# TensorE's row flags as one word of eight bits, made beside the last routing and loaded ahead of expert 0's last rows

## The chip, the cores and the metric

One core of a Trainium2 chip runs the whole program once. The metric is device time in microseconds (us). The engines are TensorE (PE in the profile, with its weight loads as PEld), VectorE (DVE), ScalarE (ACT), GpSimd (POOL) and SyncE (SP). Each runs its own list of instructions in order, and a sequencer in front of each engine reads that list: it resolves branches, loads and computes registers, and waits for semaphores.

## The reference, cut to what matters

Three steps follow each other: a gated linear attention, a dense layer, and a layer of eight experts, in which each of 3072 tokens goes to the one expert with the largest logit.

```
x = attention(q, k, v, alpha)                       # 3072 x 384
h = x @ w_in;  x = (h * cos(h)) @ w_out             # d_ff 2048
logits = x @ w_gate;  e_idx = argmax(logits, axis=1)
for e in range(8):
    mask = e_idx == e
    h  = max(x[mask] @ w1[e], 0)                    # 384 -> 1024
    ye = h @ w2[e]                                  # 1024 -> 384
    out[mask] = gate_w[mask] * eom[mask, e] * ye
```

How many tokens an expert gets is known only while the program runs.

## The kernel before

The dense layer works on groups of 512 tokens; the last one is group 5. After a group's second matmul stage the tokens are routed: `route_logits`, `route_rank` and `route_rows` (lines 488 to 541) compute for each token its row in the DRAM buffer `xs`, which has a region of rows for each expert, and keep in `base` the next free row of every expert. `route_send` scatters the rows with GpSimd's indirect DMA. After the last `route_rows`, `base - ebase` is the number of rows of each expert.

Then the experts run one after the other on up to 448 rows each (`CAP`). Expert 0 is split: its first 256 rows (`early`, written down as filled before the last group is routed) are worked on between the last routing's steps (`first(j)`, `second(j)`, lines 937 to 1003), and its last 192 rows (`r = begin(0)`) come after that: SP loads them (`load_rows`), PE transposes them (`rows_trans`, line 642), ACT and DVE split them into halves `exh` and `exl`, and the loop of line 1039 runs them as its first expert, with `e_stage1` for eight blocks `j` of nine matmuls each (line 671) and then `e_part2` for the row tiles.

An expert with at most 384 rows (`LOW`) needs less work. Whether it has that few is decided on the chip: `by_rows` (line 648) puts a branch on PE's sequencer ahead of each of the eight blocks of `e_stage1` and ahead of the 64-row tile of part two, nine branches an expert, 72 in all. The flag is in a register of PE. All eight registers are filled at line 1031: DVE computes `few` and `fewi` (lines 1023, 1026, 1030) after expert 0's last rows have been transposed, and PE loads the eight words with one load and then, for every word, two more sequencer instructions that check its bounds. The blocks of `e_stage1` write two PSUM banks in turn (`hp`), and DVE clears those two and a third one (`op`) at line 1037, just before the loop, after `fewi`.

The order is written by hand: `tc.manual_schedule` (line 937) keeps PE, ACT, DVE and SP in the order of the code, and each waits by semaphores for what it needs.

```
few_r = nc.values_load_multi_w_load_instructions(fewi[0:1, 0:E], engines=[ENG.PE], min_val=0, max_val=1)[1]
```

Of the kernel before, what the change touches and what calls it, by code (L numbers as in the profile page):

```python
# [8 lines left out]
F32 = mybir.dt.float32  # L9
F32R = mybir.dt.float32r  # L10
BF16 = mybir.dt.bfloat16
U32 = mybir.dt.uint32
# [38 lines left out]
CEB = CW8 + GU * E  # L51
CTOK = CEB + E
CROW = CTOK + NU
CCOL = CROW + 1


@with_exitstack
def kernel(
# [466 lines left out]
    def route_rows(g):  # L525
        oh, rp = rk.pop(g)
        t = s_p.tile([128, GU, E], F32, tag="rk", name="rk")
        nc.vector.tensor_tensor(
            out=t, in0=rp[:, 0], in1=base.rearrange("p (o e) -> p o e", o=1).to_broadcast([128, GU, E]), op=ALU.add
        )  # L530
        nc.vector.tensor_tensor(out=t, in0=t, in1=oh, op=ALU.mult)
        pf = s_p.tile([128, GU, 1], F32, tag="pf", name="pf")
        nc.vector.tensor_reduce(out=pf, in_=t, axis=AX.X, op=ALU.add)
        pu = s_p.tile([128, GU, 1], U32, tag="pu", name="pu")
        nc.vector.tensor_copy(pu, pf)
        nc.vector.tensor_tensor(out=base, in0=base, in1=rp[:, 1, 0], op=ALU.add)
        if g == NG - 2:

            nc.vector.tensor_scalar_max(base[:, 0:1], base[:, 0:1], float(EARLY))
        rk[g] = pu  # L540
# [404 lines left out]
    with tc.manual_schedule(engines={ENG.PE, ENG.Activation, ENG.DVE, ENG.SP}):  # L945
# [7 lines left out]
        def second(j):  # L953
            for t in range(n_t):
                e_part2(early, t, accs[t], j)
# [22 lines left out]
            x1_rows(g, s)  # L978
        route_rank(g)
        route_rows(g)  # L980
        for s in range(GU):
            route_send(g, s)
        second(1)
# [7 lines left out]
        second(5)  # L991
        first(7)
        second(6)
        m1.close()

        m2 = ExitStack()
# [12 lines left out]
        for t in range(n_t):  # L1009
# [2 lines left out]


        nt = o_p.tile([128, E + 1], F32, name="nt")
        few = o_p.tile([128, E], F32, name="few", bufs=1)
        fewi = o_p.tile([128, E], U32, name="fewi", bufs=1)
        nc.vector.tensor_tensor(out=nt[:, 0:E], in0=base, in1=ebase, op=ALU.subtract)
        nc.vector.tensor_scalar(
            out=nt[:, 0:E], in0=nt[:, 0:E], scalar1=float(127 - CAP), scalar2=127.0, op0=ALU.add, op1=ALU.max
        )  # L1020
        nc.vector.tensor_reduce(out=nt[:, E:E + 1], in_=nt[:, 0:E], axis=AX.X, op=ALU.max)

        nc.vector.tensor_scalar(
            out=few, in0=base, scalar1=float(LOW), scalar2=None, op0=ALU.subtract
        )
        nc.vector.tensor_tensor(out=few, in0=few, in1=ebase, op=ALU.is_le)
        nc.vector.tensor_copy(ntl, nt)
        nc.vector.tensor_scalar(out=ntl, in0=ntl, scalar1=7, scalar2=None, op0=ALU.logical_shift_right)

        nc.vector.tensor_copy(fewi, few)  # L1030
        few_r = nc.values_load_multi_w_load_instructions(fewi[0:1, 0:E], engines=[ENG.PE], min_val=0, max_val=1)[1]


        banks = [ps_h.tile([128, 512], F32, tag="h", name="hp") for _ in range(2)]
# [2 lines left out]
            nc.vector.memset(b, 0.0)  # L1037

        for e in range(E):
            r["few"], r["banks"] = few_r[e], banks  # L1040
            steps = load_expert(e + 1, vr_p if e % 2 else vl_p) if nxt else []

            def step():
                if steps:
                    for f in steps.pop(0):
                        f()

            hbs = []
            for j in range(NEF):

                n = r["n"]
                hb = h_p.tile([128, 2 * n], F32R, tag="hb", name="hb")
                e_stage1(r, j, hb[:, 0:n], [(slice(0, n - 64), hb[:, n + 64:]), (slice(n - 64, n), hb[:, n:n + 64])])
                hbs.append(hb)
                if j % 2:
                    step()
            r["gates"] = gates(z_p, r["xe"][:, :, DM:], len(r["tiles"]))
            n_t = len(r["tiles"])
            for i, t in enumerate((n_t - 1, *range(n_t - 1))):
                if i == n_t // 2 and nxt:  # L1060
                    rows_trans(nxt, z_p, "exh", "exl")
                step()
                if i == n_t - 1:
                    while steps:
                        step()
                ot = o_p.tile([128, DM], F32, tag="ot", name="ot")
                if r["tiles"][t] == 64:
                    op = e_acc(r, t, i, 128)
                    for m in by_rows(r.get("few"), (1, 0)):
                        if m:  # L1070
                            for j in range(NEF):
                                e_part2_both(r, t, op, j, hbs[j])
                    low = o_p.tile([64, DM], F32, tag="low", name="low", bufs=1)
                    nc.scalar.copy(low, op[64:128])
                    nc.vector.tensor_tensor(out=low, in0=op[0:64], in1=low, op=ALU.add)
                    op = low
                else:
                    op = e_acc(r, t, i)
                    for j in range(NEF):
                        e_part2(r, t, op, j)  # L1080
                e_out(r, t, op, ot)
            r = nxt
            nxt = begin(e + 2) if e + 2 < E else None
# [71 lines left out]
def _layout(inputs):  # L1155
# [32 lines left out]
    for n in range(NU):  # L1188
        c[:, CTOK + n] = (n % B) * S + (n // B) * C + perm
    c[:, CROW] = np.arange(128)  # L1190
    return {
        "units": u.reshape(NU, 128, UCOL),
        "cst": c,
# [26 lines left out]
```

## Time and profile before

| what | value |
|---|---|
| median of 3 runs | 814.5 us (813.9 to 815.12) |
| profiled execution, its own time | 812.32 us |
| its span, first to last instruction | 810.5 us |
| PE busy | 769.4 us (95%) |
| DVE, ACT, POOL busy | 501.9, 425.3, 316.6 us (62, 52, 39%) |
| mean granted TensorE clock | 0.981 of full speed |
| chain that ended last | PE 52%, issue 27%, DVE 11% |

Times are from the span's start. The last routing lies at 555 to 558 us, expert 0's last rows at 568 to 596 us, experts 1 to 7 behind them, and the end at 810.5 us. A granted clock of 1.00 is TensorE's 2.4 GHz, 0.50 its 1.2 GHz. An engine name with a q (PEldq, PEq, SPq) is the sequencer or queue in front of that engine.

### The profile page before, as it was taken

How to read it: one execution, taken by the hardware profiler on the slowest of the kernel's cores; microseconds unless marked ns; L12 is line 12 of the kernel's file. 1: busy time of each engine (PE TensorE's matmuls, PEld its weight loads, DVE VectorE, ACT ScalarE, POOL GpSimd, SP SyncE). 2: the span in 40 equal slices, each digit the busy share in tenths (PEclk: the TensorE clock that was granted, in tenths of full speed). 3: DMA queues.
4: the chain of work that ended last, by engine and by line, in shares of the span. 5: the costliest groups of instructions: out<-in, count | busy, mean ns of one | idle time of the engine just before them, and what ended most of it. 6: DMA issues, size and time to landing. Idle time of an engine off the chain costs nothing.

```text
span 810.5 us, 13963 instructions
## 1 busy us (share of the span) xinstructions
PE 769.4 (95%) x5346; PEld 655.7 (81%) x5346; DVE 501.9 (62%) x955; ACT 425.3 (52%) x782; POOL 316.6 (39%) x304
## 2 busy tenths in 40 slices
PE   8679899999999999999999999999699999999994
PEld 5557777888888888888888888889699999999994
DVE  8999998675467537663676334744565655655530
ACT  2454565754575457644665467555354545554420
POOL 3566756544355335543464424662011101101101
PEclk9998999999999999999999999999899999999998
DMA  9524452713201230113010101211565445645201
GB/s 326 205 94 159 170 199 100 243 60 112 80 1 54 73 125 1 54 59 109 31 55 20 41 0 59 89 50 44 182 192 181 135 142 176 191 123 159 67 13 34
DMA packets 46881, 85.31 MB, mean 105 GB/s; under 512 B 4152, under 2 KB 38488, under 8 KB 44240
## 3 DMA queue, kind: packets, MB, share of 16 engines
q1 hardware_dynamic: 43344, 74.67, 28.1%
q0 software_dynamic: 3456, 9.57, 3.2%
q8 instruction: 50, 0.82, 0.4%
q14 instruction: 31, 0.25, 0.1%
HBM read 69.01 MB, written 15.99 MB: 105 GB/s over the span
## 4 chain that ended last, share of the span: by engine, by line
PE 52%; issue 27%; DVE 11%; POOL 4%; DMA 2%; ACT 1%; POOLq 0%; SPq 0%; ACTq 0%; DVEq 0%
PE acc L418 22%; PE hp L379 21%; POOL out_dram L711 4%; DVE cv L347 3%; PE sc L211 2%; DMA un<-in_units_dram 2%; DVE cv L352 2%; PE yp L269 2%; PE yp L261 2%; DVE cv L356 2%; PE pp L285 1%; PE tp L442 1%; DVE t L397 1%; DVE t L392 1%; DVE w L151 1%
## 5 line engine op out<-in xcount | busy, mean ns | idle before, releaser
L405 POOL TENSOR_TENSOR gl<-t,gh 128x512 fp32r<-128x512 f32 x95 | 127.8, 1345 | 182.2 <-ACT gh L404 152.5
L386 ACT ACTIVATE t<-hp 128x512 f32<-128x512 f32 x96 | 57.3, 596 | 140.1 <-PE hp L379 130.4
L397 DVE TENSOR_TENSOR t<-hp,t 128x512 f32<-128x512 f32 x96 | 65.7, 684 | 89.3 <-ACT t L394 89.3
L392 DVE SCALAR_TENSOR_TENSOR t<-t,hp 128x512 f32<-128x512 f32 x96 | 65.7, 684 | 79.7 <-ACT t L386 79.6
L711 POOL DMA_INDIRECT out_dram<-ot,tk x32 | 31.3, 979 | 205.9 <-ACT ot L710 205.6
L687 PE MATMUL op<-h,hb 128*128 128x384 f32 x384 | 102.4, 338 | 1.7 <-PEq L654 1.7
L418 PE MATMUL acc<-gh,woh 128*128 128x512 f32 x288 | 90.3, 421 | 0.0
L677 DVE SCALAR_TENSOR_TENSOR hb<-hp,hb 128x64 fp32r<-128x64 f32 (+3 forms) x136 | 45.3, 372 | 70.1 <-ACT hb L675 70.0
L379 PE MATMUL hp<-xh,wih 128*128 128x512 f32 x288 | 83.6, 398 | 3.7 <-DVE t L397 3.1
L418 PE MATMUL acc<-gl,woh 128*128 128x512 f32 x288 | 84.2, 399 | 0.0
L418 PE MATMUL acc<-gh,wol 128*128 128x512 f32 x288 | 83.9, 399 | 0.0
L379 PE MATMUL hp<-xh,wil 128*128 128x512 f32 x288 | 82.6, 395 | 0.0
L379 PE MATMUL hp<-xl,wih 128*128 128x512 f32 x288 | 82.5, 395 | 0.0
L393 ACT ACTIVATE t<-t 128x512 f32<-128x512 f32 x96 | 60.7, 632 | 38.3 <-DVE t L392 38.3
L675 ACT ACTIVATE hb<-hp 128x448 fp32r<-128x448 f32 (+2 forms) x72 | 36.3, 504 | 72.3 <-PE hp L671 70.3
L599 DVE TENSOR_TENSOR l<-raw,h 128x768 fp32r<-128x768 f32 x60 | 57.3, 957 | 25.8 <-ACT h L595 25.0
L687 PEld LDWEIGHTS op<-h,hb 128*128 128x128 f32 x384 | 69.7, 188 | 3.0 <-issue 3.0
L394 ACT ACTIVATE t<-t,halfpi 128x512 f32<-128x512 f32 x96 | 69.6, 725 | 3.1
L379 PEld LDWEIGHTS hp<-xh,wih 128*128 128x128 f32 x288 | 54.4, 191 | 18.0 <-DVE t L397 2.2
L418 PEld LDWEIGHTS acc<-gh,wol 128*128 128x128 f32 x288 | 55.1, 191 | 13.4
L418 PEld LDWEIGHTS acc<-gl,woh 128*128 128x128 f32 x288 | 54.9, 191 | 12.8
L379 PEld LDWEIGHTS hp<-xl,wih 128*128 128x128 f32 x288 | 54.5, 189 | 12.9
(144 smaller groups left out, 1454.4 us busy)
## 6 DMA issues: line engine op xcount, KB each, us to landing
raw<-in_w_dram SPq DMA_DIRECT2D x64, 384.0 KB, 3.4
un<-in_units_dram SPq DMA_DIRECT2D x20, 1032.0 KB, 4.9
raw<-in_w_in_dram SPq DMA_DIRECT2D x16, 384.0 KB, 3.7
raw<-in_w_out_dram SPq DMA_DIRECT2D x16, 384.0 KB, 4.1
xs<-zrow SPq DMA_DIRECT2D x8, 591.0 KB, 5.8
xe<-xs SPq DMA_DIRECT2D x7, 591.0 KB, 5.1
un<-in_units_dram SPq DMA_DIRECT2D x4, 512.0 KB, 6.2
un<-in_units_dram SPq DMA_DIRECT2D x4, 256.0 KB, 6.8
```

The costliest lines, as they stand in the source:

```text
L379: nc.tensor.matmul(out=hp, lhsT=w[:, k, fs], rhs=x[:, k, :], start=(n == 0), stop=(n == 3 * KD - 1))
L386: nc.scalar.activation(out=t, in_=hps[g, j], func=ACTF.Copy, bias=MAGIC)
L392: nc.vector.scalar_tensor_tensor(out=t, in0=t, scalar=MAGIC, in1=hp, op0=ALU.subtract, op1=ALU.subtract)
L393: nc.scalar.activation(out=t, in_=t, func=ACTF.Abs)
L394: nc.scalar.activation(out=t, in_=t, func=ACTF.Sin, scale=-TWO_PI, bias=halfpi)
L397: nc.vector.tensor_tensor(out=t, in0=hps.pop((g, j)), in1=t, op=ALU.mult)
L405: eng.tensor_tensor(out=gl, in0=gf, in1=gh.bitcast(F32), op=ALU.subtract)
L418: nc.tensor.matmul(out=acc[g][k], lhsT=w[:, j, ks], rhs=a, start=(j == 0 and n == 0), stop=(j == NF - 1 and n == 2),)
L599: (nc.vector.tensor_tensor if i < 4 else sub)(out=lo, in0=raws[i], in1=h.bitcast(F32), op=ALU.subtract)
L677: nc.vector.scalar_tensor_tensor(out=out_, in0=hp[:, c], scalar=0.0, in1=hh[:, c].bitcast(F32), op0=ALU.max, op1=ALU.subtract)
L687: nc.tensor.matmul(out=op, lhsT=a[:, sl], rhs=w[:, j, :], start=(j == 0 and i == 0), stop=(j == NEF - 1 and i == 2))
L711: sent = nc.gpsimd.indirect_dma_start(out=out, out_offset=bass.IndirectOffsetOnAxis(ap=tk[0:n, t, :], axis=0), in_=ot[0:n], in_offset=None ...
```

## The change

Behind the last `route_rows`, four DVE instructions make one word: the counts `base - ebase`, then for each expert 1 or 0 by "at most 384" times a power of two from 16 new columns of the constant tile `c_sb` (eight of them used), then their sum, then the sum as an integer (`fews`). PE loads this one word behind `second(6)`, ahead of the transposes of expert 0's last rows, instead of eight words behind `second(7)`. The three DVE instructions at lines 1023, 1026 and 1030 are gone. `few >> e & 1` is written once for an expert in the loop, but the program computes it on PE's sequencer ahead of each branch: one register instruction in expert 0 (no shift), two in the others, 9 + 63 x 2 = 135 in all.

```diff
-CCOL = CROW + 1
+CPW = CROW + 1
+CCOL = CPW + 16
@@ after route_rows(g) of the last group
+        cnt = s_p.tile([128, E], F32, tag="rk", name="cnt")
+        nc.vector.tensor_tensor(out=cnt, in0=base, in1=ebase, op=ALU.subtract)
+        nc.vector.scalar_tensor_tensor(
+            out=cnt, in0=cnt, scalar=float(LOW), in1=c_sb[:, CPW:CPW + E], op0=ALU.is_le, op1=ALU.mult
+        )
+        bits = s_p.tile([128, 1], F32, tag="pf", name="bits")
+        nc.vector.tensor_reduce(out=bits, in_=cnt, axis=AX.X, op=ALU.add)
+        fews = s_p.tile([128, 1], U32, tag="pu", name="fews")
+        nc.vector.tensor_copy(fews, bits)
@@ after second(6)
+        few = nc.values_load(fews[0:1, 0:1], engines=[ENG.PE], min_val=0, max_val=(1 << E) - 1)
         m1.close()
@@ after begin(1)
-        few = o_p.tile([128, E], F32, name="few", bufs=1)
-        fewi = o_p.tile([128, E], U32, name="fewi", bufs=1)
...
-        nc.vector.tensor_scalar(
-            out=few, in0=base, scalar1=float(LOW), scalar2=None, op0=ALU.subtract
-        )
-        nc.vector.tensor_tensor(out=few, in0=few, in1=ebase, op=ALU.is_le)
         nc.vector.tensor_copy(ntl, nt)
         nc.vector.tensor_scalar(out=ntl, in0=ntl, scalar1=7, scalar2=None, op0=ALU.logical_shift_right)
-
-        nc.vector.tensor_copy(fewi, few)
-        few_r = nc.values_load_multi_w_load_instructions(fewi[0:1, 0:E], engines=[ENG.PE], min_val=0, max_val=1)[1]
...
-            r["few"], r["banks"] = few_r[e], banks
+            r["few"], r["banks"] = nc.tensor.snap((few >> e) & 1), banks
...
+    c[:, CPW:CPW + E] = 2.0 ** np.arange(E)
```

The first place is PE's list from the end of `second(6)` to the first branch of expert 0's last rows. Before, with `op` the accumulator of part two, `tp` the transposes and `ISA` the bound checks:

```order
L687 MATMUL op<-h_5168,hb 128x384
L642 MATMUL tp<-c_sb,xe 128x128 x6
L687 MATMUL op<-h_5168,hb 128x384
L687 MATMUL op<-l_5169,hb 128x384
L687 MATMUL op<-h_5168,hb 128x384 x2
L687 MATMUL op<-l_5169,hb 128x384
L687 MATMUL op<-h_5168,hb 128x384
L1031 TENSOR_LOAD fewi
L1031 ISA x16
L654 COMPARE_AND_BRANCH
```

The same stretch now (line numbers are one to ten higher):

```order
L688 MATMUL op<-h_5168,hb 128x384
L1005 TENSOR_LOAD fews
L1005 ISA x2
L643 MATMUL tp<-c_sb,xe 128x128 x6
L688 MATMUL op<-h_5168,hb 128x384
L688 MATMUL op<-l_5169,hb 128x384
L688 MATMUL op<-h_5168,hb 128x384 x2
L688 MATMUL op<-l_5169,hb 128x384
L688 MATMUL op<-h_5168,hb 128x384
L655 REGISTER_ALU
L655 COMPARE_AND_BRANCH
```

The load moved ahead of twelve matmuls, its checks went from sixteen to two, and a register instruction stands before the branch.

The second place is DVE's list around the clearing of the PSUM banks (`hp`, `op`). Before, from the split of expert 0's last rows on:

```order
L645 TENSOR_TENSOR exl<-tp,exh 128x192 x3
L630 MEMSET xe 64x394
L1017 TENSOR_TENSOR nt<-base,c_sb 128x8
L1018 TENSOR_SCALAR nt<-nt 128x8
L1021 TENSOR_REDUCE nt<-nt 128x1
L1023 TENSOR_SCALAR few<-base 128x8
L1026 TENSOR_TENSOR few<-few,c_sb 128x8
L1027 CAST ntl<-nt 128x9
L1028 TENSOR_SCALAR ntl<-ntl 128x9
L1030 CAST fewi<-few 128x8
L1037 MEMSET hp 128x512 x2
L1037 MEMSET op 128x512
```

Now:

```order
L646 TENSOR_TENSOR exl<-tp,exh 128x192 x3
L631 MEMSET xe 64x394
L1027 TENSOR_TENSOR nt<-base,c_sb 128x8
L1028 TENSOR_SCALAR nt<-nt 128x8
L1031 TENSOR_REDUCE nt<-nt 128x1
L1032 CAST ntl<-nt 128x9
L1033 TENSOR_SCALAR ntl<-ntl 128x9
L1039 MEMSET hp 128x512 x2
```

Three short instructions fewer stand ahead of the clearing of `hp`.

The third place is DVE's list behind the last routing (`pu` are the rows to scatter to, `hb` the early rows' hidden half), as it is now; before, `hb` stood right behind `base`:

```order
L536 CAST pu<-pf 128x4
L537 TENSOR_TENSOR base<-base,rp 128x8
L984 TENSOR_TENSOR cnt<-base,c_sb 128x8
L985 SCALAR_TENSOR_TENSOR cnt<-cnt,c_sb 128x8
L989 TENSOR_REDUCE bits<-cnt 128x1
L991 CAST fews<-bits 128x1
L678 SCALAR_TENSOR_TENSOR hb<-hp,hb 128x256
```

The four new instructions stand between `base` and the next work for the early rows.

## Rows read from the trace of the kernel before

**Rows 1.** The page: busy time, share and instructions of each engine.

```profile
PE 769.4 (95%) x5346; PEld 655.7 (81%) x5346; DVE 501.9 (62%) x955; ACT 425.3 (52%) x782; POOL 316.6 (39%) x304
```

**Rows 2.** PE's waits from 545 us on: total us, times, longest.

```profile
PE hp L671 <- issue: 5.4, 1, 5.4
PE op L687 <- PEq L654: 1.7, 4, 0.4
```

**Rows 3.** Timeline, 568 to 576 us: start, us, engine line op [idle before <-releaser].

```profile
568.43 0.30 PE L642 MATMUL tp<-c_sb,xe 128*128 128x128 f32 x1 [0.36 <-DMA xe<-xs]
...
570.36 0.34 PE L687 MATMUL op<-h,hb 128*128 128x384 f32 x1
...
571.40 0.16 DVE L1021 TENSOR_REDUCE nt<-nt 128x1 f32<-128x8 f32 x1
...
571.76 0.30 DVE L1027 CAST ntl<-nt 128x9 uint32<-128x9 f32 x1
572.09 0.17 DVE L1028 TENSOR_SCALAR ntl<-ntl 128x9 uint32<-128x9 uint32 x1
572.17 0.16 DVE L1030 CAST fewi<-few 128x8 uint32<-128x8 f32 x1
...
572.44 1.03 DVE L1037 MEMSET hp<- 128x512 f32 x2
573.52 0.48 DVE L1037 MEMSET op<- 128x512 f32 x1
...
576.10 0.50 PE L671 MATMUL hp<-exh,h 128*128 128x192 f32 x1 [5.40 <-issue]
```

**Rows 4.** Line 1031 on PE's sequencer: duration ns min/median/max, first, last start.

```profile
L1031 PEldq FUSED_REGOPS  x8: 146/146/160, 573.4 to 575.4; - x8
L1031 PEldq SEQ_ASSERT  x8: 18/18/28, 573.6 to 575.6; - x8
...
L1031 PEldq TENSOR_LOAD <-fewi x1: 788/788/788, 572.5 to 572.5; - x1
```

**Rows 5.** Stretches: us, busy PE PEld DVE ACT POOL, granted clock, DMA, GB/s.

```profile
576.10:581.94 5.84, 5.84 (x27) 5.84 (x28) 1.44 (x5) 1.38 (x3) 0.00 (x0) 0.50 0.17 66
581.94:587.76 5.82, 5.45 (x46) 5.21 (x46) 4.21 (x13) 3.10 (x7) 0.00 (x0) 1.00 0.43 134
```

**Rows 6.** A late load, line 1088, on PE's sequencer (columns as rows 4).

```profile
L1088 PEldq TENSOR_LOAD <-ntl x1: 332/332/332, 795.9 to 795.9; - x1
```

**Rows 7.** PE's timeline around that load.

```profile
795.73 0.51 PE L687 MATMUL op<-h,hb 128*128 128x384 f32 x2
796.07 0.33 PE L687 MATMUL op<-l,hb 128*128 128x384 f32 x1
796.25 0.51 PE L687 MATMUL op<-h,hb 128*128 128x384 f32 x2
```

**Rows 8.** Branches on PE's sequencer in one block of a later expert.

```profile
L654 PEldq COMPARE_BRANCH  x2: 65/117/169, 630.7 to 631.0; - x2
```

**Rows 9.** Semaphore waits on PE's sequencer in the same block.

```profile
L671 PEldq EVENT_SEMAPHORE  x2: 51/51/51, 630.5 to 632.1; - x2
```

**Rows 10.** PE's timeline behind two earlier idle times.

```profile
90.43 0.57 PE L222 MATMUL kp<-c_sb,un 112*128 112x112 f32 x4 [1.45 <-DVE state L302]
...
136.95 0.96 PE L379 MATMUL hp<-xh,wih 128*128 128x512 f32 x3 [1.80 <-DVE t L397]
```

**Rows 11.** Stretches around and behind those idle times (columns as rows 5).

```profile
87.05:93.00 5.95, 4.50 (x23) 3.45 (x22) 5.91 (x13) 2.72 (x6) 3.80 (x4) 1.00 0.52 179
...
138.25:141.66 3.41, 3.41 (x10) 2.63 (x9) 2.09 (x4) 2.33 (x5) 2.72 (x6) 0.50 0.66 209
```

**Rows 12.** DVE's timeline behind the last routing.

```profile
558.26 0.16 DVE L536 TENSOR_TENSOR base<-base,rp 128x8 f32<-128x8 f32 x1
561.20 0.42 DVE L677 SCALAR_TENSOR_TENSOR hb<-hp,hb 128x256 fp32r<-128x256 f32 x1 [2.79 <-ACT hb L675]
```

**Rows 13.** Timeline where expert 1 begins: DVE's split of its rows, PE's first matmul.

```profile
593.42 1.68 DVE L645 TENSOR_TENSOR exl<-tp,exh 128x448 fp32r<-128x448 f32 x3 [1.24 <-ACT exh L644]
...
596.03 0.78 PE L671 MATMUL hp<-exh,h 128*128 128x448 f32 x3
```

## The prediction

> **What bounds the kernel now.** The page comes first: PE is busy for 769.4 us of 810.5 [rows 1], so what keeps PE from its next matmul sets the time, and another engine counts only where PE waits for it. PE's waits come second. From 545 us on, where the change lies, there is one large entry: 5.4 us once, ahead of line 671, named "issue", which means that no engine held it; four times 0.4 us at the branch of line 654 come next [rows 2]. The timeline shows the place: PE's last matmul of `second(7)` starts at 570.36 us and takes 0.34, the first block of expert 0's last rows starts at 576.10, with 5.40 us of idle time between [rows 3]. Third, PE's sequencer at line 1031 fills that hole: behind DVE's `fewi` (572.17 plus 0.16 us, [rows 3]) comes the load of 788 ns, then eight register checks from 573.4 to 575.4 us [rows 4]. They are (575.4 - 573.4) / 7 = 0.29 us apart, though each lasts 0.146 and its assert 0.018, so eight cost about 2.3 us. The 5.40 us are 1.7 of waiting for `fewi`, 0.9 of load, 2.3 of checks and 0.5 of branch and start. The last view is the granted clock: it is 0.50 for the 5.84 us behind the hole and 1.00 after that [rows 5]. So the hole is paid twice, as idle time and as a slow start.
>
> **The hole.** The load, the checks and `fewi` leave it. What is late next? The first block writes the first bank that DVE clears at line 1037; before, two such clears took 1.03 us from 572.44 on, so the first ended near 572.95, hidden under the load [rows 3]. Now it decides. Three DVE instructions ahead of it are gone. `ntl` of line 1027 has to wait for the reduce of 571.40, about 0.2 us after its start as dependent DVE steps stand apart here; the next one comes 0.33 us later (572.09 - 571.76), and the clear between 0.1 and 0.27 us after that (572.44 - 572.17): it starts at 572.04 to 572.20 and ends half of 1.03 later, near 572.6 [rows 3]. With 0.2 us for the semaphore and the start, PE begins at 572.8 and not at 576.10: **3.3 us** less, and 2.1 us of the hole stay (572.8 - 570.70). Bounds: if nothing of DVE's chain moved, PE starts 0.2 us behind 572.95, 2.95 saved; if all three clears had to end (573.52 + 0.48), 1.9; 3.4 at best. I take 3.3, since only the first bank is written by block 0.
>
> **The clock.** At 0.50 PE worked on three blocks (27 matmuls) for 5.84 us; the next five blocks took 5.82, 1.16 each with the waits among them [rows 5]. Three at that pace are 3.5 us, so the slow clock costs 2.3 us now. What of it comes back depends on what 2.1 us of idle time do. Rows of this trace show both: after 1.80 us idle the clock was 0.50 for 3.41 us, after 1.45 us idle it stayed at 1.00 [rows 10, 11]. The new hole is longer than either, and 0.36 us of waiting for the rows stand shortly ahead of it [rows 3], so I expect one fall of 3.41 us. At half speed that does 1.7 us of work and costs at most 1.7; I take 1.4, for the waits on ACT and DVE in these blocks (5.82 - 5.45 = 0.37 us idle, [rows 5]) hide part. Gained: 2.3 - 1.4 = **0.9 us**; bounds are 0 (as slow as now) and 2.3 (no fall).
>
> **The load at its new place.** It needs about 1.1 us of PE's sequencer (0.79, one check of 0.29). The trace shows a load run while matmuls go on: line 1088's at 795.9 us, with PE's matmuls following each other at 795.73, 796.07 and 796.25 without a gap [rows 6, 7]. So the sequencer is ahead of the array, and the end of `second(6)` has fifteen matmuls in front of the load to cover it. Behind it the transposes wait for a DMA anyway, 0.36 us [rows 3]. Its cost is 0; the other end, if the load began only when the array is empty, is 1.1 - 0.36 = 0.7 us. I take 0, from the late load.
>
> **The four DVE steps.** They follow `base` at 558.26 us, and DVE's next work waits for ACT, 2.79 us idle [rows 12]. Four short steps of 0.2 us (0.8 us) fit in. PE wants the word only behind `second(6)`, whose transposes come at 568.43 [rows 3]. `pu`, for which the scatters wait, stands ahead of them. Cost 0; with the cover gone, 0.8 us on the early rows' path. Sixteen more columns of `c_sb` are 8 KB more in one early transfer: 0.
>
> **The 135 register instructions.** No such instruction is in the trace alone. Below zero it can't go, as nothing else is removed there. From above, take a check's 0.29 us: 39 us in all if each were exposed. What hides them is seen in a 384-row block: the sequencer gets its semaphore at 630.5 us, hands out the block, has jumped and compared by 631.0 + 0.07, and then waits until 632.1 for the next one [rows 8, 9]. So about 1 us of every block is spare, against at most 2 x 0.29 = 0.58 us. I take 0, since the wait of the row is longer than the upper price. The four 0.4 us waits [rows 2] stay: they are the jump behind an empty tile, where no register instruction is added.
>
> **The sum.** 3.3 + 0.9 = 4.2 us. Against the profiled execution that is 810.5 - 4.2 = 806.3 us of span and 812.32 - 4.2 = 808.1 of time. The profiled execution is 2.2 us below the median, so the same gain makes 814.5 - 4.2 = **810.3 us**. From expert 1 on PE runs without a large wait [rows 2], so what is gained at 573 us reaches the end.
>
> **The rivals.** *No fall of the clock.* If 2.1 us of idle time leave it at 1.00, as 1.45 us did [rows 10, 11], the whole 2.3 us come back: 814.5 - 5.6 = 808.9 us. For it speaks that the remaining hole is short; against it, the 1.80 us that sufficed. The Trainium skill ("TensorE: Matmul & The Clock Gate", section "HAM oscillation — how this bites in real kernels") gives as an abstract rule that only an idle gap above a stated length costs the clock; the new hole is shorter than that gap, so by that rule this rival would be the forecast. The trace disagrees with it, by the 1.80 us gap that was followed by 0.50.
>
> *As slow as now, or the load shows.* The clock stays at 0.50 for as much work as before, or the load costs its 0.7 us: 814.5 - 3.3 = 811.2 us, or 814.5 - 4.2 + 0.7 = 811.0.
>
> *Given back at expert 1.* DVE's split of expert 1's rows ends at 593.42 + 1.68 = 595.10, PE begins at 596.03 [rows 13]: 0.9 us spare. If expert 0 ran 4.2 us earlier and the weights of expert 1, which come by DMA and pass ACT and DVE in between, did not, all beyond 0.9 would be waited for: 813.6 us, within 0.2% (1.6 us, about what a measurement of this kernel can tell from no change). Against it: the chain to that split starts with PE's transposes and moves with them.
>
> *Slower: the register work shows.* Should the sequencer not be ahead at the blocks, each branch holds PE until its bit is made. At the shortest sequencer branch here, 65 ns [rows 8], 135 instructions cost 8.8 us: 814.5 - 4.2 + 8.8 = 819.1 us. It decides from 4.2 / 135 = 31 ns exposed for each. Against it stands the 1 us of spare time a block.
>
> **How the numbers follow.** Forecast, one fall: 0.47, 810.3 us. No fall: 0.20, 808.9. As slow as now or a visible load: 0.17, 811.1. Given back: 0.10, 813.6. Register work: 0.06, 819.1. The first three are faster by over 0.2%, 0.84; the fourth is the same, 0.10; the last slower, 0.06. The range leaves out the last two: from 808.0 (no fall and the best hole, with the 0.6 us that the three runs lie below their median) to 812.6 (a hole of only 1.9 saved).
>
> **What would show it.** The idle time ahead of line 672's first matmul falls from 5.40 to about 2.1 us, and DVE's clear of `hp` ends just before it. The load of line 1005 lies under matmuls of `second(6)` and the transposes still wait for DMA. The clock is 0.50 for about 3.4 us instead of 6.8 in this stage. The blocks of the later experts keep their pace and the four 0.4 us waits. A longer stretch between two blocks there, or a new wait named "issue" at line 672, would make the prediction wrong; so would a wait of PE for `exl` at expert 1.

## The result and the profile after

| | kernel before | changed kernel |
|---|---|---|
| median | 814.71 us (813.9 to 815.12, 4 runs) | 807.97 us (805.62 to 808.92, 4 runs) |
| profiled execution, its span | 812.32, 810.5 us | 805.62, 803.8 us |
| mean granted clock | 0.981 | 0.988 |

The ratio is 0.9914 [0.9891, 0.9937]: 6.7 us faster. The forecast was 4.2 us faster, 810.3 us, with a range from 808.0 to 812.6. The sign was right and the size was not; the measured time lies at the very edge, 0.03 us below the range. The three repeats below have medians of 806.54 to 807.76 us and lie below it too.

The page of the changed kernel, its span, PE's busy time and the chain by engine; beside [rows 1]:

```profile
span 803.8 us, 14087 instructions
PE 764.3 (95%) x5346; PEld 651.9 (81%) x5346; DVE 502.1 (62%) x956; ACT 425.2 (53%) x782; POOL 316.6 (39%) x304
PE 54%; issue 26%; DVE 10%; POOL 4%; DMA 3%; ACT 1%; POOLq 0%; SPq 0%; ACTq 0%; DVEq 0%
```

PE is still the bound. It was busy for 5.1 us less (769.4 - 764.3) with the same matmuls, so not all of the gain is idle time that went: some matmuls ran at the higher clock or stand closer. Of the 6.7 us between the two profiled spans, 1.1 lie ahead of the changed stretch: the first 256-column block of expert 0 starts at 546.09 us before and at 545.03 after. The timeline of PE, where the hole of [rows 3] was (start, duration, operation, then the idle time before it and what ended that):

```profile
567.20 0.30 PE L643 MATMUL tp<-c_sb,xe 128*128 128x128 f32 x1
567.67 0.74 PE L643 MATMUL tp<-c_sb,xe 128*128 128x128 f32 x5 [0.17 <-DMA xe<-xs]
...
569.11 0.34 PE L688 MATMUL op<-h,hb 128*128 128x384 f32 x1
571.76 0.55 PE L672 MATMUL hp<-exh,h 128*128 128x192 f32 x3 [2.32 <-DVE ntl L1033]
```

The hole is 2.32 us instead of 5.40, and a DVE line ends it instead of "issue". DVE's timeline of the changed kernel, around the four new steps and then around the hole:

```profile
557.24 0.15 DVE L537 TENSOR_TENSOR base<-base,rp 128x8 f32<-128x8 f32 x1
557.42 0.17 DVE L984 TENSOR_TENSOR cnt<-base,c_sb 128x8 f32<-128x8 f32 x1
...
558.02 0.15 DVE L991 CAST fews<-bits 128x1 uint32<-128x1 f32 x1
560.23 0.42 DVE L678 SCALAR_TENSOR_TENSOR hb<-hp,hb 128x256 fp32r<-128x256 f32 x1 [2.06 <-ACT hb L676]
...
570.17 0.16 DVE L1031 TENSOR_REDUCE nt<-nt 128x1 f32<-128x8 f32 x1
570.37 0.45 DVE L1032 CAST ntl<-nt 128x9 uint32<-128x9 f32 x1
570.85 0.17 DVE L1033 TENSOR_SCALAR ntl<-ntl 128x9 uint32<-128x9 uint32 x1
571.13 1.02 DVE L1039 MEMSET hp<- 128x512 f32 x2
```

The four steps take 0.8 us and DVE still waits 2.06 us for ACT behind them, where it waited 2.79 [rows 12]. At the hole the first of the two clears ends near 571.13 + 0.51 = 571.64, and PE starts at 571.76: what is late now is the clear of the first bank. Where a wait has two ends close together, the name in the bracket (`ntl` here, `hp` in other profiles below) may be the instruction just ahead of it.

PE's sequencer at the load, by line 1005 (operation, count, duration in ns as minimum, median and maximum, first and last start):

```profile
L1005 PEldq TENSOR_LOAD <-fews x1: 484/484/484, 564.9 to 564.9; - x1
L1005 PEldq FUSED_REGOPS  x1: 165/165/165, 565.5 to 565.5; - x1
L1005 PEldq SEQ_ASSERT  x1: 32/32/32, 565.7 to 565.7; - x1
```

It is through at 565.8 us, while PE works on its matmuls until 567.1 and then starts the first transpose without a wait that the load could have made. The stretch of the first blocks, as [rows 5] (window; its length; busy time and instructions of PE, PEld, DVE, ACT, POOL; granted clock; DMA share; GB/s):

```profile
571.76:572.56 0.80, 0.80 (x7) 0.80 (x8) 0.74 (x2) 0.00 (x0) 0.36 (x1) 1.00 0.99 294
572.56:575.97 3.41, 3.41 (x18) 3.41 (x18) 0.96 (x5) 1.09 (x3) 0.00 (x0) 0.50 0.92 330
575.97:582.14 6.17, 5.83 (x51) 5.55 (x50) 4.52 (x13) 3.39 (x8) 0.00 (x0) 1.00 0.44 129
```

In this profile it is one fall of 3.41 us, as forecast; in the profile of before the fall lasted 6.83 us (575.15 to 581.98), of which 5.84 lay in the blocks [rows 5].

What the forecast did not have is at expert 1. Its eight blocks of nine 448-column matmuls, first and last group of three, before:

```profile
596.03 0.78 PE L671 MATMUL hp<-exh,h 128*128 128x448 f32 x3
...
610.29 0.78 PE L671 MATMUL hp<-exh,l 128*128 128x448 f32 x3
```

and after:

```profile
590.57 0.77 PE L672 MATMUL hp<-exh,h 128*128 128x448 f32 x3
...
604.54 0.77 PE L672 MATMUL hp<-exh,l 128*128 128x448 f32 x3
```

From the first group to the last it is 14.26 us before and 13.97 after, with the same work and no wait of PE in either. From start to start two of these matmuls are 207 ns apart before and 203 after. Experts 6 and 7, the others with more than 384 rows, show the same (201 and 203 ns); the 384-column matmuls of experts 2 to 5 do not change.

### The profile page after: what moved, and what is told of

The parts are those of the page before. It is cut to its first block, busy times and chain, and to the rows that moved or that the text cites. A ratio compares the mean times of both kernels' runs of the same rounds, so it can differ in the third digit from the quotient of the medians.

```text
span 803.8 us, 14087 instructions
## 1 busy us (share of the span) xinstructions
PE 764.3 (95%) x5346; PEld 651.9 (81%) x5346; DVE 502.1 (62%) x956; ACT 425.2 (53%) x782; POOL 316.6 (39%) x304
## 4 chain that ended last, share of the span: by engine, by line
PE 54%; issue 26%; DVE 10%; POOL 4%; DMA 3%; ACT 1%; POOLq 0%; SPq 0%; ACTq 0%; DVEq 0%
PE acc L419 22%; PE hp L380 21%; POOL out_dram L712 4%; DVE cv L348 2%; PE sc L212 2%; PE yp L270 2%; PE yp L262 2%; DVE cv L353 2%; DMA un<-in_units_dram 1%; DVE cv L357 1%; PE pp L286 1%; PE tp L443 1%; DVE w L152 1%; DVE t L398 1%; DVE t L393 1%
```

## The experiments

Each comparison had its own runs of the kernel before, whose median was 812.9 to 813.5 us. Taken together, 52 runs of before have a median of 813.4 us (810.47 to 815.26) and 22 of the change one of 807.6 (805.44 to 809.86): 5.8 us, less than the 6.7 of the first comparison. Stages below run from the start of one matmul to that of another.

**The change again.** The same kernel, three more times.

> The changed kernel itself, timed again beside the kernel before. Theory (three terms: the hole of 5.40 us cut to 2.3, one fall of the clock instead of two, and 448-column matmuls that stand 0.202 us apart instead of 0.207, three experts x 72 x 0.005 = 1.0 us): about 3.1 + 1.4 + 1.0 = 5.5 us faster than before, the hole 2.3 us and the 448-column matmuls again 0.202 us apart. Rival (the part beyond the forecast 4.2 us is luck of the clock in the stages ahead of the change): 4.2 us faster, and the spacing of 0.202 us does not come back.

807.54 us, ratio 0.9933 [0.9914, 0.9952]; hole 2.31 us, one fall of 3.41 us, the 448-column matmuls at 203, 201 and 203 ns. The time does not tell the theory from the rival (5.4 us, with an interval from 3.9 to 7.0); the spacing does, and it belongs to the kernel, not to the execution.

> The changed kernel once more, for a further profile of the stretch behind the hole. Theory (how long the clock stays at 0.50 behind the 2.3 us hole differs from execution to execution, 3.41 or 6.83 us, and the time scatters with it): hole 2.3 us again, the 72 matmuls of the 192-row blocks in 10.4 us with a fall of 3.41 us or in 11.5 to 12.1 us with one of 6.83; time 807 to 808.5 us, ratio 0.991 to 0.9945. Rival (the length goes with the program): 3.41 us and 10.4 us again, ratio 0.9933 as before.

807.76 us, 0.9927 [0.9912, 0.9941]; hole 2.32 us, fall of 3.41 us, which the theory and the rival both allow.

> The changed kernel, fourth profile. Theory (where the fall begins and how long it lasts differs from execution to execution): hole 2.3 us; a fall of 3.41 us that begins within 1.5 us of the first block, or one of 6.83 us that begins at the block or more than 1.5 us behind it. Rival (in this program it is always 3.41 us): 3.41 us once more, wherever it begins. Ratio 0.9915 to 0.994 in both.

806.54 us, 0.9932 [0.9912, 0.9951]. The hole was there, and the clock did not fall behind it. The timeline of PE in change_3:

```profile
572.74 0.55 PE L672 MATMUL hp<-exh,h 128*128 128x192 f32 x3 [2.31 <-DVE hp L1039]
```

and its windows, over all eight 192-row blocks:

```profile
572.74:581.79 9.05, 8.62 (x71) 8.20 (x72) 6.08 (x18) 4.48 (x10) 0.36 (x1) 1.00 0.63 212
```

The granted clock is 1.00 throughout, and the blocks take 9.05 us instead of 10.37. One and the same program with one and the same idle time of 2.3 us was followed by a fall in three profiles and by none in the fourth. So "one fall" and the rival "no fall" were both right, in different executions; the theory and the rival of this run both had a fall in them and both failed. The Trainium skill ("TensorE: Matmul & The Clock Gate", section "HAM oscillation — how this bites in real kernels") gives as its abstract rule that idle gaps above a stated length are to be avoided, and 2.3 us is shorter than that length; that the clock then stays up held in one profile of four.

**The kernel before again.** Two more profiles of it.

> The kernel before once more, for a second profile of it. Theory (the hole and the 448-column spacing belong to the program, the clock's falls in the first 140 us and the length behind the hole to the execution): hole 5.2 to 6.1 us, 448-column matmuls of experts 1, 6 and 7 at 206.6 ns, 192-row blocks in 10.6 to 11.7 us. Rival (the 206.6 ns were chance of one execution): another spacing, near 202 ns.

> The kernel before, a third profile. Theory (the stretch up to 545 us differs from execution to execution with the falls of the clock, and the profiles of before shown so far, 812.32 and 810.94 us, are quick ones of a kernel with a median of 813 to 814.7): a slower one here has its first 256-column block of this stretch later, at 546 to 549 us, and the stretch from there on takes 263.8 to 264.5 us as in the others. Rival (the stretch behind 545 us is what scatters): 545 to 547 us, and more than 265 us from there on.

The hole was 5.75 us in both, the fall 6.83 us, the 192-row blocks took 10.78 and 10.83 us, and the spacing was 207 ns in all three experts. The hole and the spacing belong to the program, as the theory of before_2 has it. before_3 took 263.9 us from 545 us on, as its theory has it, but at 812.58 us it lies below the median again, so it tells little of the stretch ahead of that.

The two profiles also bear on the row from which the forecast of the clock was taken, 1.80 us of idle time and then a granted clock of 0.50 [rows 10, 11]. The same idle time in before_2, and the stretch behind it:

```profile
137.32 0.95 PE L379 MATMUL hp<-xh,wih 128*128 128x512 f32 x3 [1.83 <-DVE t L397]
...
137.32:143.00 5.68, 5.68 (x25) 4.64 (x26) 2.81 (x5) 4.29 (x8) 5.40 (x8) 1.00 0.56 185
```

Here, and in before_3, the clock stayed at 1.00. In all 19 profiles of this document this idle time is 1.75 to 1.85 us; a fall of 3.41 us begins within 1.4 us behind it in eleven of them (one of three of the kernel before, two of four of the change), and none does in eight.

**Layout: the constants alone.** The kernel before with 16 unused columns more in `c_sb`.

```diff
-CCOL = CROW + 1
+CCOL = CROW + 1 + 16
```

> The kernel before with 16 unused columns more in the constant tile and nothing else: every tile behind it in the same pool side lies 64 bytes further per partition. Theory (the spacing of the 448-column matmuls comes from where tiles lie): 0.202 us apart as in the changed kernel, about 1.0 us faster than before, the hole still 5.4 us. Rival (the spacing comes from the branches, the loads or the shorter list of VectorE): 0.207 us and no change of the time.

812.85 us, ratio 0.9998 [0.9986, 1.001]: no gain in time. The spacing of the change came in two experts of three (203, 201 and 207 ns; 0.68 us less in sum). Expert 1 in wide_constants, 14.05 us from the first group to the last:

```profile
596.49 0.76 PE L671 MATMUL hp<-exh,h 128*128 128x448 f32 x3
...
610.54 0.78 PE L671 MATMUL hp<-exh,l 128*128 128x448 f32 x3
```

In the profile 0.17 us of it went in the 256-column blocks (120 ns instead of 117) and 0.24 in a longer way to the first 192-row block (the hole was 6.03 us). The theory was right on the spacing and missed the time.

**Layout: the change without it.** The powers of two stand in columns of `c_sb` that are no longer used by then, GpSimd writes them, and the places of `few` and `fewi` stay reserved. All tiles lie as before the change.

```diff
-CPW = CROW + 1
-CCOL = CPW + 16
+CCOL = CROW + 1
@@ ahead of the last group
+        for i in range(E):
+            nc.gpsimd.memset(c_sb[:, CT + i:CT + i + 1], float(1 << i))
@@ beside ntl
+        o_p.tile([128, E], F32, name="few", bufs=1)
+        o_p.tile([128, E], U32, name="fewi", bufs=1)
```

> The change without its layout: the powers of two are written into eight dead columns of the constant tile by GpSimd early in the program, the tile keeps its old width, and the places of few and fewi stay reserved. Theory: hole 2.3 us, one fall of the clock, 448-column matmuls 0.207 us apart, 4.5 us faster than before (3.1 + 1.4). Rival (layout does nothing): 0.202 us apart and 5.5 us faster, as the changed kernel.

808.26 us, ratio 0.9945 [0.9924, 0.9966], 4.5 us below before. Hole 2.31 us. Expert 1's blocks in word_old_layout, on PE's timeline:

```profile
594.97 0.78 PE L671 MATMUL hp<-exh,h 128*128 128x448 f32 x3
...
609.23 0.78 PE L671 MATMUL hp<-exh,l 128*128 128x448 f32 x3
```

14.26 us again. With everything of the change but the new places in memory the spacing is that of before, and the gain is close to the 4.2 us of the forecast. The theory had one short fall of the clock; it lasted 6.83 us in this profile. The times alone do not show what the layout is worth: the interval of word_old_layout, 2.8 to 6.2 us faster, overlaps that of `again`, 3.9 to 7.0. The spacing in the traces shows it.

**Layout: which tile.** In the kernel before, 64 bytes lie between the output tiles and those of `hb`; and the change with 48 more columns instead of 16.

```diff
+        gap_p = m2.enter_context(tc.tile_pool(name="gap_p", bufs=1, side="left"))
+        gap = gap_p.tile([128, 16], F32, name="gap")
+        nc.gpsimd.memset(gap, 0.0)
         h_p = m2.enter_context(tc.tile_pool(name="h_p", bufs=10, side="left"))
```

> The kernel before with a tile of 64 bytes a partition that lies between the output tiles and those of hb (it is cleared once by GpSimd): only hb's tiles move, by 64 bytes, and the rows' tiles stay. Theory (where the rows' tiles exh and exl lie sets the spacing, which TensorE reads as moving operand in these blocks): 207 ns in experts 1, 6 and 7, 14.87 us each, as before. Rival (where hb's tiles lie, which ACT and DVE write meanwhile): 201 to 203 ns in at least one of the three. The hole stays at 5.2 to 6.1 us in both.

Expert 1 in only_hb_64:

```profile
596.96 0.77 PE L671 MATMUL hp<-exh,h 128*128 128x448 f32 x3
...
611.03 0.78 PE L671 MATMUL hp<-exh,l 128*128 128x448 f32 x3
```

14.07 us: expert 1 moved to 203 ns although the rows' tiles had not moved, as the rival has it; experts 6 and 7 stayed at 207. So the rows' place alone does not decide it, and neither does that of `hb` alone: in the change `hb` lies where it did before. A wider `c_sb` also moves the weights of the odd experts (`vl_p`), but not those of expert 6, which lie on the other side (`vr_p`); expert 6 went to 201 ns all the same. Tiles for loads and outputs (`raw`, `cv`) move with `c_sb` too, and no run moved those alone. 813.66 us, one run.

> The change with 48 more columns of c_sb instead of 16, so that the rows' tiles lie 192 bytes and hb's 128 bytes behind where they lay before. Theory (the place within 128 bytes counts): as 64 and 0 bytes in the change, so 14.6, 14.4 and 14.6 us for the 72 matmuls of experts 1, 6 and 7. Rival (another distance counts): between 14.67 and 14.87 us, as with 128 bytes. The hole stays at 2.3 us.

203, 201 and 207 ns; the blocks took 14.59, 14.56 and 14.88 us: partly as 64 bytes, partly as before. No rule by the distance comes out of it. 809.54 us, one run; PE waited 1.1 us for the rows' DMA there.

**The place of the load.** The word is made early but loaded at the old place, once more on another chip.

```diff
-        fews = s_p.tile([128, 1], U32, tag="pu", name="fews")
+        fews = c_sb[:, CPW + E:CPW + E + 1].bitcast(U32)
@@ the load moves from behind second(6) to behind ntl, after second(7)
+        few = nc.values_load(fews[0:1, 0:1], engines=[ENG.PE], min_val=0, max_val=(1 << E) - 1)
```

> The word is made at the early place, as in the change, but loaded at the old place, behind second(7) and the instructions of ntl. Theory (what made the hole was that the load had to wait for a value of DVE's last chain, and eight checks): the word is ready 10 us before, so PE's sequencer goes to the load as soon as it has handed out second(7); 0.8 us of load and one check end before DVE has cleared the first bank. Idle time ahead of line 672 about 2.3 us as in `again` (2.31), one fall of the clock, time within 1 us of the change (ratio to the kernel before 0.993). Rival (the place ahead of the rows is what counts): the load and its check, 0.5 to 1.1 us, are added to the hole: 2.8 to 3.4 us idle, and the clock is at 0.50 for 6.83 us instead of 3.41: 1.0 to 2.5 us slower than the change, ratio 0.9945 to 0.9965.

> word_old_place once more. It had the same hole of 2.31 us as the change, but the clock was at 0.50 for 6.83 us and its ratio was 0.9955. Theory (chance of the execution): 3.41 or 6.83 us, and beside change_2 on the same chip within 0.8 us of it. Rival (loading at the old place makes the slow stretch longer): 6.83 us again, 192-row blocks in 11.5 to 12.1 us, and 1.2 to 2 us above change_2.

The hole was 2.31 and 2.32 us. PE's sequencer in the first of them:

```profile
L1033 PEldq TENSOR_LOAD <-c_sb x1: 487/487/487, 570.1 to 570.1; - x1
L1033 PEldq FUSED_REGOPS  x1: 165/165/165, 570.6 to 570.6; - x1
```

The load is done at 570.9 us, three microseconds ahead of PE's first block at 573.99. So the hole does not need the early place: it needs a word that does not hang on DVE's last chain. In time it was 809.99 us (0.9955 [0.9941, 0.9969]) and then 808.37 us (0.9929 [0.9909, 0.995]) beside 807.76 of change_2. The first result is the rival's, the second is not; in both profiles the clock was at 0.50 for 6.83 us, and whether that is chance, as in the change, stays open. The window of the first profile:

```profile
574.00:580.83 6.83, 6.83 (x32) 6.83 (x33) 3.08 (x9) 1.71 (x4) 0.35 (x1) 0.50 0.52 183
```

**Eight flags instead of a word.** Made early, no register instructions in the branches, loaded at the new place or at the old one.

```diff
-        few = nc.values_load(fews[0:1, 0:1], engines=[ENG.PE], min_val=0, max_val=(1 << E) - 1)
+        few_r = nc.values_load_multi_w_load_instructions(fewi[0:1, 0:E], engines=[ENG.PE], min_val=0, max_val=1)[1]
...
-            r["few"], r["banks"] = nc.tensor.snap((few >> e) & 1), banks
+            r["few"], r["banks"] = few_r[e], banks
```

> Eight flags as before the change, but made early and loaded at the change's place ahead of expert 0's last rows; no register instructions in the branches. In `again` PE's sequencer stands about 2.3 us ahead of the array there. Theory (the lead is all the cover there is): the load of 0.79 us and eight checks 0.29 us apart need 3.1 us instead of 0.8 to 1.1, so the transposes of the rows come later: about 0.5 to 1 us of new idle time ahead of line 642, beyond the wait for DMA, and the time is 0.5 to 1 us above the change. Rival (covered, since the transposes wait for DMA anyway): the transposes start as in the change, the time is that of the change, or below it by what the register instructions cost (0 if they are hidden).

808.92 us, ratio 0.9947 [0.9933, 0.9961]. PE's sequencer at the load:

```profile
L1001 PEldq FUSED_REGOPS  x8: 146/146/160, 567.0 to 569.0; - x8
...
L1001 PEldq TENSOR_LOAD <-fewi x1: 797/797/797, 566.1 to 566.1; - x1
```

and PE's timeline behind it:

```profile
569.41 0.87 PE L643 MATMUL tp<-c_sb,xe 128*128 128x128 f32 x6 [1.10 <-issue]
```

The checks end at 569.2 and the transposes start at 569.41 behind "issue": the sequencer's lead is used up, and PE stands for 1.1 us. In the change the DMA of the rows let it stand there for 0.17 to 1.05 us, so only a part of the 1.1 us is new. From the last 256-column matmul to the first 192-row block it is 6.65 us here and 5.97 to 6.61 us in the four profiles of the change. By the ratios the kernel is 1.1 to 1.6 us slower than the change, with intervals that overlap, and this profile has a fall of 6.83 us, with 11.98 us for the 192-row blocks. So the theory holds on the place (one word fits into the lead, eight do not), but what that costs in time is not shown.

> Eight flags, no word and no register instructions in the branches; they are made early, as the word in the change, and loaded at the old place behind second(7). Theory (only that the load hung on DVE's last chain made the hole): in word_old_place the load began 3.3 us ahead of the first matmul behind the hole; load and eight checks take 0.8 + 8 x 0.29 = 3.1 us, so they just fit under DVE's clear: hole 2.3 to 2.6 us, time within 1 us of change_3. Rival (eight checks are too long there): hole 2.9 us or more, at least 0.6 us above change_3.

809.31 us, 0.995 [0.9937, 0.9964], 2.8 us above change_3 in the medians and 1.7 us above the 22 runs of the change. PE's sequencer there:

```profile
L1029 PEldq FUSED_REGOPS  x8: 146/146/160, 573.6 to 575.6; - x8
...
L1029 PEldq TENSOR_LOAD <-c_sb x1: 2117/2117/2117, 571.4 to 571.4; - x1
```

and PE's timeline:

```profile
576.30 0.55 PE L672 MATMUL hp<-exh,h 128*128 128x192 f32 x3 [3.31 <-DVE op L1035]
```

The hole is 3.31 us. The load took 2.1 us where eight words took 0.8 in [rows 4], so the checks end at 575.8 and not near 574.5, and PE starts 0.5 us behind them, as it did before. The `op` in the bracket is only the instruction that ended close by: in the changed kernel the first block starts at 571.76 us, ahead of the clear of `op` at 572.21. The rival holds, and packing is worth 1.0 us of the hole in this pair of runs. It hangs on the long load: after one of 0.8 us the checks would have ended ahead of the clear of the first bank, near 575.2, and why the load took 2.1 us is open.

**More register work.** Forty more operations on the bit ahead of each branch, which leave it as it is.

```diff
-            r["few"], r["banks"] = nc.tensor.snap((few >> e) & 1), banks
+            flag = (few >> e) & 1
+            for _ in range(20):
+                flag = (flag + 1) >> 1
+            r["few"], r["banks"] = nc.tensor.snap(flag), banks
```

> The change with 40 more register operations on the bit ahead of each of the branches of expert 0 to 7 (they leave the bit as it is); the compiler makes of them 7 fused instructions a branch. One fused instruction took 0.165 us on PE's sequencer behind the load, one register operation about 0.04. Theory (some 1 us a block is spare, so the change's 0.1 us costs nothing): 7 x 0.165 = 1.2 us or more a block no longer fits in the blocks of 1.16 us of expert 0 nor quite in those of 1.55 us: the waits of the sequencer for its semaphore vanish and the matmuls of the blocks move apart by 0.2 to 1 us a block, 64 blocks: 10 to 60 us slower than the change. Rival (the sequencer runs ahead far enough, or these instructions do not hold it): within 1 us of the change; then the rival of the prediction on register work could not have come true at any size near its price.

823.47 us, ratio 1.0124 [1.0108, 1.0139]. PE's sequencer at the branches:

```profile
L655 PEldq FUSED_REGOPS  x504: 93/122/152, 569.7 to 794.4; - x168
L655 PEldq ALU_OP  x135: 36/36/42, 569.6 to 793.2; - x135
L655 PEldq COMPARE_BRANCH  x108: 67/174/343, 570.9 to 794.5; - x108
```

and PE's timeline at expert 2:

```profile
635.44 0.77 PE L672 MATMUL hp<-exh,h 128*128 128x384 f32 x3 [0.17 <-issue]
...
637.42 0.77 PE L672 MATMUL hp<-exh,h 128*128 128x384 f32 x3 [0.17 <-issue]
```

That is 15.8 us above the 22 runs of the change, in the range of the theory. From the first register instruction to the branch it is 1.3 us (570.9 - 569.6). Expert 2's eight 384-row blocks took 15.55 us where they take 13.47 in `again`. The first two lost nothing; from the third on a block takes about 2.0 us (637.42 - 635.44) where it takes 1.6 in `again`, so about 0.35 us is exposed. So about 1.0 us a block is covered, the spare time that was read from [rows 8, 9]. In the change the same line shows 135 `ALU_OP` of 36 to 42 ns, far below that.

**The hole filled.** Eleven matmuls that nobody reads, in the hole.

```diff
+        for _ in range(11):
+            nc.tensor.matmul(out=banks[4][:, :DM], lhsT=ew[0][0][:, 0, 0:128], rhs=ew[0][2][:, 0, :], start=True, stop=True)
```

> The change with 11 matmuls of 384 columns that nobody reads, put into the hole behind second(7) (11 x 0.17 = 1.9 us of the 2.3 idle); the blocks' start stays bound by DVE's clear. Theory (the fall of the clock is caused by the idle time, and costs about 1.4 us behind the hole): idle time below 0.6 us, no fall of the clock at expert 0's last rows, the 72 matmuls of the 192-row blocks in 9.6 us instead of 10.5 to 11.6, time 0.9 to 1.9 us below the change. Rival (the clock falls for another reason, or the time of these blocks is bound by ACT and DVE): the fall stays or the stage takes as long, time within 0.4 us of the change.

807.31 us, ratio 0.9926 [0.9912, 0.9939]. The windows over the 192-row blocks:

```profile
575.00:584.06 9.06, 8.63 (x72) 8.21 (x72) 6.08 (x18) 4.48 (x10) 0.36 (x1) 1.00 0.70 237
```

The clock stayed at 1.00 and the blocks took 9.06 us, as the theory has it; the time is that of the change, as the rival has it. Since the change itself has such executions (change_3), one profile without a fall does not tell them apart. What filling the hole brings in the mean is below what these runs resolve.

**The banks earlier.** Banks 0 and 1 are taken and cleared ahead of expert 0's last rows, only the third at the old place; then the same with 32 columns instead of 16.

```diff
+        banks = [ps_h.tile([128, 512], F32, tag="h", name="hp") for _ in range(2)]
+        for b in banks:
+            nc.vector.memset(b, 0.0)
         r = begin(0)
         rows_trans(r, z_p, "exh", "exl")
...
-        for b in banks[:3]:
-            nc.vector.memset(b, 0.0)
+        nc.vector.memset(banks[2], 0.0)
```

> The changed kernel with the first two PSUM banks cleared ahead of the transposes of expert 0's last rows instead of behind VectorE's counts. Theory (what is left of the hole is VectorE's list up to the clear of the first bank): the 2.3 us shrink to 0.2, the granted clock stays at 1.00 there, and the time is 2.1 + 1.4 = 3.5 us below the changed kernel, 9 us below before. Rival (another wait stands just behind the clear, ScalarE's or the weights' of expert 1): the hole keeps 1.5 us or more, or the blocks wait as long, and less than 1 us is gained over the changed kernel.

805.69 us, ratio 0.991 [0.9891, 0.993], the fastest kernel here. PE's timeline:

```profile
572.23 0.77 PE L643 MATMUL tp<-c_sb,xe 128*128 128x128 f32 x5 [0.98 <-DVE xe L631]
...
573.88 0.48 PE L672 MATMUL hp<-exh,h 128*128 128x192 f32 x3
...
576.67 0.55 PE L672 MATMUL hp<-exh,h 128*128 128x192 f32 x3 [0.64 <-DVE hb L678]
```

The hole is gone: the first block follows the last matmul of `second(7)` directly. So DVE's clear was what held PE in the changed kernel. Of the 2.3 us some came back as new waits: the early clears stand ahead of the clear of `xe`, for which the transposes now wait 0.98 us, and the blocks catch up with DVE (0.64 us). The granted clock stayed at 1.00, as the theory has it, and the 192-row blocks took 9.53 us with these waits. Over the change's three ratios (0.9927 to 0.9933) it gains 1.4 to 1.9 us, where the theory said 3.5 and the rival below 1.

> banks_early (the change, with banks 0 and 1 taken and cleared ahead of the rows), and c_sb wider by 32 columns (128 bytes of each partition) instead of 16, so that all that lies behind it moves by 64 bytes more. Theory (what sets the spacing of the 448-column matmuls is where their tiles lie within 128 bytes): the tiles lie as before the change in that respect, so the spacing is 206.6 ns again, 1.0 us more in experts 1, 6 and 7, time 806.7 us where banks_early had 805.7. Rival (something else that c_sb's width moves, or any shift will do): spacing 200 to 203 ns as in banks_early, the same time.

806.22 us, ratio 0.9911 [0.9895, 0.9927]; 206, 203 and 207 ns, 0.6 us more than banks_early in the three experts. Neither theory as it stood: most of the spacing of before is back, but not in full.

## Why the prediction was wrong in size

Stages from the first 256-column block of expert 0 to the end of the span, mean of three profiles of before and four of the change, in us:

| stage | before | change | gained | forecast |
|---|---|---|---|---|
| 256-column blocks | 20.64 | 20.80 | -0.15 | 0 |
| from there to the first 192-row block | 9.53 | 6.35 | 3.2 | 3.3 |
| 192-row blocks | 11.05 | 10.04 | 1.0 | 0.9 |
| experts 1, 6 and 7 | 92.89 | 91.90 | 1.0 | 0 |
| all else | 129.91 | 129.88 | 0.0 | 0 |
| sum | 264.0 | 259.0 | 5.1 | 4.2 |

**The hole: right.** The step from load and checks to the clear of the first bank is what happened, and banks_early shows that the clear is what is late. 2.1 us were forecast to stay and 2.3 did: from `ntl`'s cast to the next instruction it was 0.48 us (570.85 - 570.37) where 0.33 had been reckoned from [rows 3]. That the stage still came out near 3.3 is in part luck: the forecast started from a hole of 5.40 us, and the two other profiles of before had 5.75.

**The clock: right in the mean, wrong as a number.** 0.9 us were taken and 1.0 came, which is luck as much as reckoning. The term is a spread: 10.37, 10.37, 10.38 and 9.05 us for the blocks of the change, 11.55, 10.78 and 10.83 us before, and 11.5 to 12.0 us in four profiles of variants with the same hole and a fall of 6.83 us. The forecast treated one fall as a property of the program and gave "no fall" 0.20 as a rival; they are draws of the same program. So was the row behind it: the fall after 1.80 us did not come in before_2 and before_3. And the trace of before has a gap that speaks against taking 1.45 us as short enough: PE stood for 1.40 us ahead of its matmul at 81.92 us, and the clock was 0.50 from 83.64 us on, for 3.41 us.

**The load, the DVE steps, the register work: right.** The load is hidden, though the word has less to spare than "fifteen matmuls" suggested: eight_early used up the lead with 2.2 us more. The four DVE steps cost nothing. The register work is hidden by about 1.0 us a block.

**The step that failed** is the sentence "Sixteen more columns of `c_sb` are 8 KB more in one early transfer: 0." It counted the transfer and not the place: each tile allocated behind `c_sb` on that side lies 64 bytes further on, and with `few` and `fewi` gone the tiles of `hb` come back to where they were. That is worth 1.0 us in experts 1, 6 and 7, against 0.15 lost in the 256-column blocks; word_old_layout, which has everything else, shows 207 ns and a gain of 4.5 us. So the move of the tiles is shown to be the cause of the spacing; what meets there is not known. The trace of before could not have given the size, but it had a sign that something there could move: its 256-column matmuls stand 117 ns apart and its 384-column ones 174, and on the line through both, an estimate, 448 columns would take 202.5 and not 207. The term should have had bounds on both sides, and the low end of the range would have lain about a microsecond lower.

**The anchor.** The sum was set against a median of three runs, 814.5 us; 52 runs give 813.4. That 1.1 us too is more than the 0.03 by which the range was missed: set against 813.4, the same terms would have put the measured time inside it, with the layout still at nothing. The low end itself was written down as 808.0, while its terms give 814.5 - 3.4 - 2.3 - 0.6 = 808.2. Of the 5.8 us between the medians of all runs, the stages place 5.1. The other 0.7 us is not placed: the start of the first 256-column block shows no difference (545.3 to 546.9 us in three profiles of before, 545.0 to 546.9 in four of the change), and all three profiles of before are quicker than its median. It may be chance; it was not shown.

The rivals "given back at expert 1" and "register work slower" did not occur. That a late split would hold PE at expert 1 is refuted by the blocks' start at 590.57 us without a wait.

## What to carry to other kernels

A value that a sequencer needs should be made well before, so that its load hangs on no chain, and packed, so that load and checks fit into the sequencer's lead (0.9 us did here, 3.1 did not); then look at what is late next, since here the clear of a bank, moved up in its turn, was worth another 1.4 to 1.9 us. Count a moved or widened tile as an edit of every tile behind it, with a price that can have either sign. Treat the clock behind an idle gap of about 2 us as a spread of executions, and take more than one profile before calling a fall or its absence an effect of the change.

## What the runs showed of the hardware that was not expected

- Matmuls of 448 columns without any wait stood 207 ns apart in one layout and 201 to 203 in another, with tiles moved by 64 bytes of a partition. Distances of 64, 128 and 192 bytes and tiles of both kinds (rows, `hb`) all changed it, in some experts and not in others. Which accesses meet there was not found.
- The same program with the same 2.3 us of idle time showed the granted clock at 0.50 for 3.41 us in three profiles and not at all in a fourth; variants with the same idle time showed 6.83 us. Behind 1.75 to 1.85 us of idle time at 137 to 139 us, eleven profiles showed a fall of 3.41 us and eight none.
- A load of eight words to PE's sequencer took 0.79 and 0.80 us in two kernels and 2.12 in a third, where the words were read from `c_sb` behind `second(7)`; one word took 0.48 to 0.49. Why the 2.12 is open.
- A register operation on PE's sequencer took 36 to 42 ns. Of 1.3 us of such work in front of each block of nine 384-column matmuls about 0.35 us was exposed, so some 1.0 us was covered.
